# Reordering the opening of a fused attention and feed-forward kernel: an earlier first norm, feed-forward products in place of fills, three loads on GpSimd's queue

## The chip, the cores and the metric

The kernel runs on one core of a Trainium2 chip. The metric is device time in microseconds of one execution. A core has five engines that run independently and meet through semaphores: TensorE (matmuls, "PE" in the profile, with its weight loads as "PEld"), VectorE ("DVE"), ScalarE ("ACT"), GpSimd ("POOL") and SyncE ("SP", which only issues DMAs here). Each engine executes its own instructions in the order in which the program lists them. An instruction that has to wait holds up everything behind it on its engine, and nothing on the others.

## The reference

For 8 batches of 12 heads, 448 tokens and 64 features per head, q and k are divided by their norms, and attention is taken over the cosines:

```python
q_n = q / (np.linalg.norm(q, axis=-1, keepdims=True) + 1e-06)
k_n = k / (np.linalg.norm(k, axis=-1, keepdims=True) + 1e-06)
scores = np.matmul(q_n, k_n.transpose(0, 1, 3, 2)) / tau      # tau = 0.1
attn = softmax(scores)
x = np.matmul(attn, v)                  # (8, 12, 448, 64) -> (3584, 768)
h = x @ w_in                            # 768 -> 2048
g = np.maximum(0.01 * h, h)
out = g @ w_out                         # 2048 -> 768
```

Inputs and outputs are float32; products are taken in bf16.

## The kernel before, in words

**Slots.** A pair of heads is the unit of the first two batches: slots 0 to 5 are the six pairs of batch 0, slots 6 to 11 those of batch 1. From slot 12 (`OLD`) on, slots come two to a unit (one for q, one for k) in another layout. Every slot goes through the same steps, each on its own engine:

1. `load_qk(s)` brings q and k into a buffer `qk_h` (four buffers, so slot s takes the one of slot s-4). Slots below 12 need four DMAs (lines 142 to 145), later ones two (line 134). All are on SyncE's queue, apart from three at the very start.
2. `squares(s)` on GpSimd (line 206 for slots below 12, line 199 later), `sums(s)` on VectorE (220, 214), `roots(s)` on ScalarE (227, 228), `normalise(s)` on VectorE (236, 237, then 253 or 243), which writes `qn`.
3. `transposes(s)`: for slots below 12 seven matmuls on TensorE (267) and a copy on VectorE (308).
4. `scores(s, key tiles)`: matmuls (329) and one exponential per key tile on ScalarE (338).
5. For two slots together (a quad j): `totals(j)` sums the exponentials on TensorE and inverts the sums on ScalarE (360, 361), `products(j, e)` multiplies by v (349), and `scale(j, e)` on VectorE (380) writes two of the six 128-row tiles of `xT`. `attend(j)` is all three.

`hold(x)` is a one-element copy on GpSimd (585). It keeps GpSimd's next squares behind the named `qn`.

**Feed-forward.** `first(c, m)` makes one 128-row tile of h from six matmuls (`KT` = 6, line 474) and an activation on ScalarE (483). `second(c, ts, half)` needs 16 matmuls with one half of w_out's columns (505). `work[0]` lists the 16 `first` and 6 `second` groups of the first chunk; `feed_groups(0, n)` issues the next n of them between attention steps. Of its last six groups three use w_out's first half and then three its second half.

**Order.** The order is written out by hand: a loop over the six slots of batch 0 (line 621), then straight lines for slots 6 to 15 (from line 688), then a planned stream. Before it stand a few lines for slot 0 (589 to 617). `fill(n)` issues n matmuls of 512 columns on a constant tile (576), whose results nobody reads.

**GpSimd's queue.** GpSimd computes the squares, and it also issues the loads that change float32 to bf16: `load_v(j)` (160), `load_v_rem(b)` (168, one DMA per head position), `load_w_in(i)` (105, quarters), `load_w_out(half)` (111). Such a load is an instruction in GpSimd's order of work like any other.

**PSUM.** `banks(n)` hands out one or two of eight banks, the longest unused first; a bank with a name in `kept` isn't handed out until `given_back`.

Of the kernel before, what the change touches and what calls it, by code (L numbers as in the profile page):

```python
# [16 lines left out]
def kernel(  # L17
# [10 lines left out]
    nc = tc.nc  # L28
# [8 lines left out]
    NPAIR = H // 2  # L37
    NSLOT = B * NPAIR
    NQ = NPAIR // 2
# [83 lines left out]
            x[:, 512:896].rearrange("p (h t d) -> p h t d", h=2, d=D),  # L123
        )

    def load_qk(s, engs=(nc.sync, nc.sync), rem_engs=None):
        if s >= NSLOT:
            return
        whole = ldp.tile([128, 14 * D], F32, name="qk_h")
        if s >= OLD:  # L130
            u, which = divmod(s - OLD, 2)
            for w, pair in enumerate(UNITS[u][1]):
                b, h0 = pair // NPAIR, 2 * (pair % NPAIR)
                nc.sync.dma_start(
                    out=whole[64 * w : 64 * w + 64],
                    in_=(q, k)[which][b, h0 : h0 + 2].rearrange("h (p t) d -> (h p) (t d)", t=14),
                )
            raw[s] = whole
            return
        b, h0 = s // NPAIR, 2 * (s % NPAIR)  # L140
        q_h, k_h = halves(whole)
        engs[0].dma_start(out=q_h[:, :, 0:3], in_=main(q, b, h0, 2))
        engs[1].dma_start(out=k_h, in_=main(k, b, h0, 2))
        for i, (x, eng) in enumerate(zip((q, k), rem_engs or engs)):
            eng.dma_start(
                out=q_h[64 * i : 64 * i + 64, :, 3],
                in_=x[b, h0 : h0 + 2, MAIN:S].rearrange("h p d -> p h d"),
            )
        raw[s] = (q_h, k_h)
# [315 lines left out]

    begun = {}

    def first(c, m, lo=0, hi=KT):
        c0, n = chunk_cols(c)
        if c not in hT:  # L470
            hT[c] = htp.tile([128, MT, 512], BF16, name="hT")
        pm = begun.pop((c, m)) if lo else banks(1)
        for kt in range(lo, hi):
            nc.tensor.matmul(  # L474
                out=pm[:, :n],
                lhsT=w_in_sb[:, kt, m * 128 : (m + 1) * 128],
                rhs=xT[c // 2][:, kt, c0 : c0 + n],
                start=(kt == 0), stop=(kt == KT - 1),
            )
        if hi < KT:  # L480
            begun[c, m] = pm
            return
        nc.scalar.activation(out=hT[c][:, m, :n], in_=pm[:, :n], func=AF.Prelu, alpha=0.01)  # L483

    osb = {}
# [112 lines left out]
        )  # L598
    roots(0)
    squares(1, (nc.scalar, gp))  # L600
    sums(1, (1,))
    normalise(0)
    load_qk(4)
    load_v_rem(0, range(2))
    hold(qn[0][:, 6, 0, 0:1])
# [15 lines left out]
    for s in range(NPAIR):  # L621
        j = s // 2 - 1 if s >= 2 else None
        even = s % 2 == 0
        n = s + 2 if 0 < s < NPAIR - 2 else None
        last = s == NPAIR - 1
        if s == 1:
            roots(2)
        scores(s, (0,))
        if j is not None and not even:
            products(j, 1)  # L630
        scores(s, (1,))
        fill(2)
        if n:
            sums(n, (0,))
        if not last:
            normalise(s + 1)
            load_qk(s + 5)
        if late:
            scale(late.pop(), 1)
        if j is not None and not even:  # L640
            scale(j, 0)
        if last:
            load_w_out(0)
        else:
            hold(qn[s + 1][:, 6, 0, 0:1])
        squares(s + 3)
        if s == 0:
            sums(2)
            load_v_rem(0, range(2, 4))
        if s in (1, 2):  # L650
            load_v(s)
        if last:
            load_v(NQ)
            load_v_rem(1)
        elif s != 1:
            load_w_in(max(s - 1, 0))
        if n:
            sums(n, (1,))
        scores(s, (2,))
        if not even or s == 0:  # L660
            fill(2)
        if n and not even:
            roots(n)
        if not even:
            scores(s, (3,))
        if j is not None and even:
            totals(j)
        if not last:
            transposes(s + 1)
        if j is not None and even:  # L670
            products(j, 0)
        if not even or s == 0:
            fill(2)
        if n and even:
            roots(n)
        if j is not None and not even:
            late.append(j)

    def attend(j):
# [8 lines left out]
    deals["apart"] = False  # L688
    deals["width"] = 64
    s, j = NPAIR, NQ - 1  # L690
    scale(late.pop(), 1)
    totals(j)
    sums(s)
    po = banks(2)
    for e in range(2):
        products(j, e, po[:, e])
    for m in range(2):
        first(0, m, 0, KT - 2)
    for e in range(2):
        scale(j, e)  # L700
    roots(s)
    for m in range(2):
        first(0, m, KT - 2)
    work[0] = work[0][2:]
    normalise(s)
    load_qk(s + 4)
    hold(qn[s][:, 6, 0, 0:1])
# [2 lines left out]
    feed_groups(0, 1)  # L710
    transposes(s)
    roots(s + 1)
    feed_groups(0, 1)
    normalise(s + 1)
    load_qk(s + 5)
    sums(s + 2)
# [4 lines left out]
    roots(s + 2)  # L721
    normalise(s + 2)
    hold(qn[s + 2][:, 6, 0, 0:1])
    squares(s + 4)
    load_v(s // 2 + 1)
    load_w_out(1)
# [4 lines left out]
    transposes(s + 2)  # L731
    roots(s + 3)
    normalise(s + 3)
    load_qk(s + 6)
    sums(s + 4)
    feed_groups(0, 2)
    scores(s + 1, (2, 3))
# [23 lines left out]
    feed_groups(0, 1)  # L761
    transposes(s + 4)
    sums(s + 5)
    feed_groups(0, 2)
    roots(s + 5)

    scores(s + 3, (0, 1, 2))
# [7 lines left out]

    scores(s + 4, (0, 1))
    scores(s + 3, (3,))
    load_qk(s + 9)
    settle(s + 6)
    sums(s + 7)  # L780
    feed_groups(0, 1)
# [3 lines left out]
    scores(s + 5, (0, 1))  # L785
    feed_groups(0, 1)
    attend(NQ + 1)
    load_qk(s + 10)
    settle(s + 7)
    sums(s + 8)  # L790

# [146 lines left out]
```

## Time and profile before

| | |
|---|---|
| median of 3 runs | 422.45 us (421.23, 422.45, 1805.44) |
| the profiled execution | 421.03 us |
| its span, first to last instruction | 419.2 us |
| TensorE busy | 410.0 us, 98% of the span |
| ScalarE, VectorE, GpSimd busy | 254.4, 223.0, 116.6 us |
| granted TensorE clock | 1.000 of full speed |
| first half of w_out, issue to landing | 24.5 us |
| second half of w_out, issue to landing | 20.7 us |

The profile shows one execution. Busy times are those in which an engine executes an instruction. A row of the timeline reads: start and duration in us, engine, line, operation, tile written and tiles read, how many in a row; in brackets the idle time of the engine just before and what ended it. A row of the list of waits reads: who waited, for whom, us in total, how often, the longest. The one run of 1805.44 us lies far from the others, and the profiled execution agrees with the two lower ones.

### The profile page before, as it was taken

To read this page: it belongs to the slowest core of one execution; us is meant where nothing else is said; L and a number is where in the kernel's file an instruction comes from. 1 tells how busy PE (TensorE), PEld (TensorE's weight loads), DVE (VectorE), ACT (ScalarE), POOL (GpSimd) and SP (SyncE) were. 2 spreads that over 40 slices of the span, in tenths; PEclk is the share of its full clock that TensorE was granted. 3 is DMA by queue.
4 is the path that set the end of the run, shared out by engine and by line. 5 is a ranking of instruction groups with operands and counts; after the bars stand their busy time and mean duration, and the time that the engine had idled before them with its cause. 6 is when DMAs were issued, how large, how long until landed. Compare 5 with 4: busy or idle time off the path is not lost.

```text
span 419.2 us, 11328 instructions
## 1 busy us (share of the span) xinstructions
PE 410.0 (98%) x4797; PEld 211.9 (51%) x4797; DVE 223.0 (53%) x385; ACT 254.4 (61%) x430; POOL 116.6 (28%) x149
## 2 busy tenths in 40 slices
PE   7899999999999999999999999999999999999996
PEld 2334555544455555544455555554445555654563
DVE  6886886874687555864583864464621311210021
ACT  4896877377766686757874778547764364014300
POOL 3877472431433223512430523131210000000000
PEclk9999999999999999999999999999999999999999
DMA  6999999485387932884275592743441100010021
GB/s 164 173 232 231 221 236 225 107 238 113 84 196 224 215 79 57 203 205 115 60 181 160 126 233 74 170 121 89 90 89 52 66 38 3 38 77 0 2 75 75
DMA packets 41906, 53.82 MB, mean 128 GB/s; under 512 B 12544, under 2 KB 32256, under 8 KB 41856
## 3 DMA queue, kind: packets, MB, share of 16 engines
q1 hardware_dynamic: 25680, 40.88, 34.9%
q0 software_dynamic: 15488, 11.80, 19.8%
q8 instruction: 37, 0.61, 0.6%
q10 hardware_dynamic: 688, 0.43, 0.4%
q14 instruction: 13, 0.11, 0.1%
HBM read 45.61 MB, written 11.01 MB: 135 GB/s over the span
## 4 chain that ended last, share of the span: by engine, by line
PE 89%; DMA 3%; DVE 3%; ACT 3%; issue 0%; SPq 0%; DVEq 0%
PE ps L505 35%; PE ps L474 33%; PE ps L425 9%; PE ps L400 7%; PE ps L349 3%; DMA qk_h<-in_q_dram 3%; DVE qn L253 2%; ACT pe L338 1%; PE ps L329 1%; PE ps L576 1%; DMA qk_h<-in_k_dram 1%; PE ps L267 1%; ACT ss L227 0%; ACT hT L483 0%; ACT norms L228 0%
## 5 line engine op out<-in xcount | busy, mean ns | idle before, releaser
L505 PE MATMUL ps<-w_out_sb,hT 128*128 128x384 bf16 x896 | 151.3, 326 | 0.4 <-DVE xT L380 0.4
L474 PE MATMUL ps<-xT,w_in_sb 128*128 128x384 bf16 (+1 forms) x768 | 150.8, 353 | 0.0
L406 ACT ACTIVATE pe<-ps 128x896 bf16<-128x896 f32 x126 | 108.9, 915 | 44.6 <-PE ps L400 44.6
L505 PEld LDWEIGHTS <-hT 128*128 128x128 bf16 x896 | 85.5, 98 | 65.2 <-issue 10.3
L474 PEld LDWEIGHTS <-w_in_sb 128*128 128x128 bf16 x768 | 72.8, 98 | 74.0 <-issue 9.2
L483 ACT ACTIVATE hT<-ps 128x384 bf16<-128x384 f32 (+1 forms) x128 | 67.6, 550 | 54.1 <-PE ps L474 53.6
L516 DVE COPY osb<-ps 128x384 f32<-128x384 f32 (+1 forms) x56 | 30.8, 551 | 101.3 <-PE ps L505 100.3
L199 POOL TENSOR_TENSOR sq<-qk_h 128x896 f32<-128x896 f32 x36 | 60.5, 1681 | 3.3 <-DMA qk_h<-in_k_dram 3.2
L585 POOL CAST seen<-qn 128x1 f32<-128x1 bf16 x46 | 8.9, 193 | 173.7 <-DVE qn L243 168.0
L243 DVE TENSOR_TENSOR qn<-qk_h,r 128x896 bf16<-128x896 f32 x36 | 42.5, 1182 | 1.4 <-DVE r L237 0.2
L338 ACT ACTIVATE pe<-ps 128x896 bf16<-128x896 f32 x42 | 35.9, 915 | 2.4 <-PE ps L329 2.3
L214 DVE TENSOR_REDUCE ss<-sq 128x14 f32<-128x896 f32 x36 | 37.3, 1037 | 0.0
L400 PE MATMUL ps<-qkT 64*32 64x448 bf16 x1008 | 36.5, 353 | 0.0
L236 DVE TENSOR_REDUCE r<-norms 128x14 f32<-128x28 f32 x48 | 8.6, 179 | 49.2 <-ACT norms L228 48.7
L227 ACT ACTIVATE ss<-ss,tiny 128x14 f32<-128x14 f32 x48 | 14.7, 306 | 28.5 <-DVE ss L214 25.6
L450 DVE TENSOR_TENSOR xT<-ps,rb 128x448 bf16<-128x448 f32 x32 | 18.4, 617 | 22.3 <-PE ps L425 21.2
L289 DVE STREAM_TRANSPOSE tt<-qn 128x448 f32<-128x448 f32 x36 | 29.6, 821 | 0.9
L425 PE MATMUL ps<-pe,vq 64*32 64x448 bf16 x1008 | 27.0, 349 | 0.0
L206 POOL TENSOR_TENSOR sq<-qk_h 128x384 f32<-128x384 f32 (+1 forms) x21 | 20.8, 1009 | 14.9 <-DMA qk_h<-in_k_dram 14.9
L400 PEld LDWEIGHTS <-qkT 64*32 64x32 bf16 x1008 | 13.2, 91 | 19.3 <-issue 14.5
L425 PEld LDWEIGHTS <-vq 64*32 64x32 bf16 x1008 | 14.5, 93 | 8.0 <-issue 0.3
L253 DVE TENSOR_TENSOR qn<-qk_h,r 128x512 bf16<-128x512 f32 (+1 forms) x24 | 18.2, 798 | 0.4
(52 smaller groups left out, 215.8 us busy)
## 6 DMA issues: line engine op xcount, KB each, us to landing
qk_h<-in_q_dram SPq DMA_DIRECT2D x36, 224.0 KB, 4.3
qk_h<-in_k_dram SPq DMA_DIRECT2D x36, 224.0 KB, 4.4
out_dram<-osb SPq DMA_DIRECT2D x20, 384.0 KB, 3.0
qkT<-tt SPq DMA_DIRECT2D x72, 56.0 KB, 3.3
qkT<-tt SPq DMA_DIRECT2D x36, 112.0 KB, 3.5
vq<-in_v_dram POOLq DMA_DIRECT2D x16, 224.0 KB, 5.1
w_in_sb<-in_moe_w_in_dram POOLq DMA_DIRECT2D x4, 768.0 KB, 11.1
w_out_sb<-in_moe_w_out_dram POOLq DMA_DIRECT2D x2, 1536.0 KB, 22.6
```

Source lines behind the costliest of these rows:

```text
L199: gp.tensor_tensor(sq, raw[s], raw[s], op=ALU.mult)
L214: nc.vector.tensor_reduce(ss[s], sqs[s].rearrange("p (t d) -> p t d", d=D), axis=AX.X, op=ALU.add)
L243: nc.vector.tensor_tensor(qn[s].rearrange("p m d e -> p m e d"), raw[s].rearrange(f"p ({t[1:-1]} d) -> p m e d", e=n, d=D), r.rearrange(f" ...
L289: nc.vector.transpose(out=to.rearrange(("p g (c m) -> p m g c", "p g (m c) -> p m g c")[which], m=7), in_=qn[s].bitcast(F32).rearrange("p ...
L338: nc.scalar.activation(out=dst, in_=sc[:, :, :S], func=AF.Exp, scale=inv_tau)
L400: nc.tensor.matmul(out=sc[32 * strip : 32 * strip + 32, a, :S], lhsT=x[rows, c0 : c0 + 32], rhs=x[rows, 0:S], start=True, stop=True,)
L406: nc.scalar.activation(out=pq[u, i], in_=sc[:, :, :S], func=AF.Exp, scale=inv_tau)
L425: nc.tensor.matmul(out=po[32 * strip : 32 * strip + 32, w, :S], lhsT=weights, rhs=pq[us[x if two else 0], i][rows, a, :], start=(i == 0), ...
L474: nc.tensor.matmul(out=pm[:, :n], lhsT=w_in_sb[:, kt, m * 128 : (m + 1) * 128], rhs=xT[c // 2][:, kt, c0 : c0 + n], start=(kt == 0), stop= ...
L483: nc.scalar.activation(out=hT[c][:, m, :n], in_=pm[:, :n], func=AF.Prelu, alpha=0.01)
L505: nc.tensor.matmul(out=po2[:, :HALF], lhsT=hT[c][:, m, ts * 128 : (ts + 1) * 128], rhs=w_out_sb[:, m, half * HALF : (half + 1) * HALF], st ...
L516: nc.vector.tensor_copy(out=o[:, half * HALF : half * HALF + cut], in_=po2[:, :cut])
```

## The change

In the lines for slot 0 and in the loop over batch 0:

- `normalise(0)` stands ahead of `sums(1, (1,))`, both on VectorE.
- `scores(s, (0,))` stands ahead of `roots(2)` in step s = 1, and `sums(2)` in step 0 stands behind `transposes(1)`.
- In step s the loop lists the load of slot s+4 instead of s+5 (step 0 still loads slot 5, step 1 none, step 5 loads slot 9).
- w_in's second quarter is loaded in step 1, ahead of v's third load, instead of in step 2, behind it.
- In step 5 two fills of two matmuls each go. In their place stand matmuls of the first two feed-forward groups: first the k tiles 0 and 2 of both groups, then the tiles 1 and 3. `first` takes a list of k tiles for that, and its bank is kept until the group is complete. `scale(j, 1)` is issued directly behind `scale(j, 0)`.

In the straight lines behind the loop:

- Groups 2 and 3 are begun where groups 0 and 1 were, and all four are completed together. Two calls of `feed_groups` are shortened by one group each, so that the number of groups stays 22.
- The load of slot 12 is issued by GpSimd instead of SyncE, behind `hold` of slot 8. There too stand the load of v for quad 3 and the four `load_v_rem(1)`, which were in step 5; all of them are ahead of `squares(10)`.
- The loads of slots 15 and 16 are issued by GpSimd instead of SyncE, in their old places in the program.

```diff
-    def first(c, m, lo=0, hi=KT):
+    def first(c, m, kts=range(KT)):
...
-        pm = begun.pop((c, m)) if lo else banks(1)
-        for kt in range(lo, hi):
+        if (c, m) in begun:
+            pm, done = begun.pop((c, m))
+        else:
+            pm, done = banks(1, (c, m, "begun") if len(kts) < KT else None), 0
+        for i, kt in enumerate(kts):
...
-                start=(kt == 0), stop=(kt == KT - 1),
+                start=(done + i == 0), stop=(done + i == KT - 1),
...
+    normalise(0)
     sums(1, (1,))
-    normalise(0)
...
+        scores(s, (0,))
         if s == 1:
             roots(2)
-        scores(s, (0,))
...
-            load_qk(s + 5)
+        if s == 0:
+            load_qk(5)
+        elif s > 1:
+            load_qk(s + 4)
...
         if last:
+            scale(j, 1)
             load_w_out(0)
...
         if s == 0:
-            sums(2)
             load_v_rem(0, range(2, 4))
...
-        if last:
-            load_v(NQ)
-            load_v_rem(1)
-        elif s != 1:
-            load_w_in(max(s - 1, 0))
+        if s < 2:
+            load_w_in(s)
+        elif 2 < s < NPAIR - 1:
+            load_w_in(s - 1)
...
         scores(s, (2,))
-        if not even or s == 0:
+        if last:
+            for m in range(2):
+                first(0, m, (0, 2))
+        elif not even or s == 0:
             fill(2)
...
             transposes(s + 1)
+        if s == 0:
+            sums(2)
...
+        if last:
+            for m in range(2):
+                first(0, m, (1, 3))
+        elif not even or s == 0:
             fill(2)
...
-    for m in range(2):
-        first(0, m, 0, KT - 2)
+    for m in range(2, 4):
+        first(0, m, range(KT - 2))
...
-    for m in range(2):
-        first(0, m, KT - 2)
-    work[0] = work[0][2:]
+    for m in range(4):
+        first(0, m, range(KT - 2, KT))
+    work[0] = work[0][4:]
...
     roots(s + 1)
-    feed_groups(0, 1)
     normalise(s + 1)
...
     hold(qn[s + 2][:, 6, 0, 0:1])
+    load_qk(s + 6, eng=gp)
+    load_v(NQ)
+    load_v_rem(1)
     squares(s + 4)
     load_v(s // 2 + 1)
     load_w_out(1)
...
     normalise(s + 3)
-    load_qk(s + 6)
     sums(s + 4)
...
     sums(s + 5)
-    feed_groups(0, 2)
+    feed_groups(0, 1)
     roots(s + 5)
...
-    load_qk(s + 9)
+    load_qk(s + 9, eng=gp)
...
-    load_qk(s + 10)
+    load_qk(s + 10, eng=gp)
```

In the straight lines s is 6, so s + 6 is slot 12, s + 9 is slot 15, s + 4 is slot 10.

## The prediction

> **What bounds the kernel now.** I read the page's busy times first, then who TensorE waits for, then GpSimd's order of work between 36 and 70 us, then the landings of single loads.
>
> ```profile
> PE 410.0 (98%) x4797; PEld 211.9 (51%) x4797; DVE 223.0 (53%) x385; ACT 254.4 (61%) x430; POOL 116.6 (28%) x149
> ...
> PE 89%; DMA 3%; DVE 3%; ACT 3%; issue 0%; SPq 0%; DVEq 0%
> ```
>
> TensorE is busy for all but 9.2 us. What can be gained is thus small whatever is moved: less TensorE work, or fewer of those 9.2 us. Work added anywhere else costs only where TensorE comes to wait.
>
> ```profile
> PE ps L576 <- DVE pe L559: 1.6, 1, 1.6
> PE ps L267 <- DVE qn L253: 1.0, 1, 1.0
> PE ps L329 <- ACT pe L338: 0.8, 3, 0.3
> PE ps L329 <- ACT norms L228: 0.8, 1, 0.8
> PE ps L329 <- DVE qkT L308: 0.6, 2, 0.3
> PE ps L505 <- DVE xT L380: 0.4, 1, 0.4
> ```
>
> All of these but the last lie before 28 us. After that TensorE hardly waits, but it is not far ahead of the others. The transposes of slots 8, 9 and 10 (L267 at 47.66, 51.84, 55.40) take some 0.64 us from their first matmul to the next group, where those of slot 7 took 0.39: their second half starts when DVE's qn ends (55.79 for slot 10, matmuls at 55.85). So the chain load, squares (GpSimd), sums, roots, qn runs without slack there, and GpSimd sits in it:
>
> ```profile
> 39.22 0.81 POOL L160 DMA_DIRECT2D v_b<-in_v_dram  x1
> 40.03 2.49 POOL L168 DMA_DIRECT2D v_rem<-in_v_dram  x4
> 42.51 0.55 POOL L585 CAST seen<-qn 128x1 f32<-128x1 bf16 x1
> 45.23 1.82 POOL L206 TENSOR_TENSOR sq<-qk_h 128x512 f32<-128x512 f32 x2 [2.17 <-DMA qk_h<-in_k_dram]
> 48.14 0.18 POOL L585 CAST seen<-qn 128x1 f32<-128x1 bf16 x1 [1.09 <-DVE qn L253]
> 50.40 2.53 POOL L206 TENSOR_TENSOR sq<-qk_h 128x512 f32<-128x512 f32 x2 [2.08 <-DMA qk_h<-in_k_dram]
> 52.88 0.82 POOL L160 DMA_DIRECT2D v_b<-in_v_dram  x1
> 53.69 1.16 POOL L111 DMA_DIRECT2D w_out_sb<-in_moe_w_out_dram  x1
> 55.86 0.18 POOL L585 CAST seen<-qn 128x1 f32<-128x1 bf16 x1 [1.00 <-DVE qn L253]
> 56.04 1.82 POOL L206 TENSOR_TENSOR sq<-qk_h 128x512 f32<-128x512 f32 x2
> 58.04 0.82 POOL L160 DMA_DIRECT2D v_b<-in_v_dram  x1 [0.18 <-issue]
> ```
>
> The third load of v and the four v_rem of 39.22 to 42.52 stand where GpSimd then idles 2.17 us for slot 9. The change puts them, and slot 12's two loads, between 48.33 and the squares of slot 10. The last row holds the second point: the trace has the queue's wait for that load ending at 57.53, and the first half of w_out landed at 57.51 (24.5 us after its issue at 32.98). GpSimd's loads use eight completion semaphores in turn, in every one of the 24 loads whose semaphores I followed, and a load waits until the one eight places before it has landed. v's sixth load stands eight behind w_out's first half.
>
> **Part by part.**
>
> *First norm earlier.* DVE idled 1.04 us until 7.26 for GpSimd's squares; norms(0) were ready at 6.81. So DVE's run to the copy of qkT(0) starts 0.4 earlier, and the first scores start near 9.9 instead of 10.35. Then sums(2) goes behind the copy of qkT(1): that copy starts at 12.55 instead of 13.69 and the second pair's scores at 13.2 instead of 14.36. But roots(2) now follow the first exponential (13.6 to 14.5) and end at 15.0 instead of 14.36; qn(2) ends at 16.66 (was 16.45), sums(3) at 17.13 (was 16.92), roots(3) start at 17.15 (was 17.17), and the fourth exponential of this pair, behind them on ScalarE, at 17.6 (was 17.64). The next one starts at 18.46, was 18.57. I take 0.1 us; the ends are 0 and 2.2 (0.8, 0.8 and 0.6 of the waits above).
>
> *Loads of slots 6 to 9 one place later in the program.* Nothing: SyncE issues only these loads there, in the same order, when the buffer's last reader is done (slot 6 at 16.52, qn(2) ends at 16.45).
>
> *w_in's second quarter ahead of v's third load.* GpSimd's transfers land in order of issue without a pause from 16 to 74 us (25.44, 27.26, 30.06, 34.78, 40.10, 43.92, 57.51). Exchanging the third and fourth gives w_in near 32.0 and v at 34.8; their readers come at 33.6 and 35.1. Zero, and up to 1 us of waiting that the later wait would cover.
>
> *Fills become products.* In the last step two fills of 0.54 us (33.56 to 34.10) go, and eight matmuls of 0.163 (16 in 2.61) come: 0.22 us more. ScalarE's last exponential ends at 34.60 and held the last part of the totals to 34.68, so this is nearly covered. Afterwards these eight are saved: 1.08 us less TensorE work in all. By scores(6) six groups are done instead of five, and the groups taken out later give them back, so TensorE is some 0.1 us early until 56 and 1.1 after it. scale(1,1) runs in the same place on DVE (31.70). The kept banks are ones long read.
>
> *GpSimd, 48 to 53 us.* After hold(8) (48.33) come two loads of slot 12, v (0.82) and four v_rem (2.49). No row has the slot's load on GpSimd; the nearest are vq (0.62, also 64 partitions) and SyncE's 0.49; at most w_out's 1.2. With 0.62 each: 4.55 us. The squares of slot 10 start at 52.9, not 50.40, last 1.83 beside an idle DVE (2.53 before), and end at 54.7 instead of 52.93: +1.8. Sums, roots, qn follow at their old distances: qn(10) ends at 57.6, the transposes at 57.8 instead of 56.03. One group (0.98) less stands behind them, so scores(9) start at 58.8 (was 58.07).
>
> *GpSimd's next loads.* v's fifth load is now eight behind w_out's first half and goes out at 57.5 at the earliest; w_out's second half is eight behind slot 12's first load, which lies behind w_out in GpSimd's transfers. Its 224 KB need less than v's 2.68 (57.51 to 60.19) and more than a v_rem's 0.3; by bytes read (v is read as 393 KB) 1.6, so 59.1. w_out's issue takes 1.2, hold(10) 0.2: the squares of slot 11, behind all this on GpSimd, start at 60.5 instead of 56.04, **+4.45**. From there by the old distances: squares end 62.3, sums 62.9, roots 63.55, qn(11) at 65.9 (it ran beside the next squares, as before), transposes(11) end at 66.15 instead of 61.93. TensorE finishes the group ahead of them at 62.1 and waits. **+4.2 us**; all later work is TensorE's own, back to back, and keeps it.
>
> *Slots 15 and 16 on GpSimd.* They land behind w_out's second half: near 78 and 80 instead of 68.77 and 74.23. Their squares come at 76.64 + 4.2 = 80.8 and 84.9. Zero. w_out itself: slot 12 until 60.6, v 63.3, v_rem 64.5, v 66.8 (their old steps of 2.68, 1.18, 2.27), then 10.7 as before or less, 77.5 at most; read at 74.44 + 4.2 = 78.6. Zero, with 1.1 us to spare.
>
> A rule to set beside the wait: TensorE would stand idle some 3.3 us before transposes(11). At the start the trace shows what follows idleness: weight loads of the fill 0.43 us apart from 2.00 to 4.13, and 0.215 later, so half speed for the first 2.9 us. The Trainium skill (TensorE: Matmul & The Clock Gate, "Part 1: The HAM clock gate") says that about 3.4 us of idling halves the clock until some 3.4 us of work have passed; by an estimate from it 1.7 us would come on top. The trace of before has no later gap that long (the granted clock is 1.00 throughout). This is a rival below, priced from the rows.
>
> **The sum.** The profiled execution took 421.03 (span 419.2, 1.8 around it). 421.03 + 4.2 = 425.2. Ordinary runs took 421.23 and 422.45, so I add 0.2: **425.4**.
>
> **The rivals.**
>
> 1. *The clock falls after the wait.* For: 3.3 us of idling. Against: no such row after the start. Price: 2.9 us at half speed, 1.45: 426.9.
> 2. *The eight-place wait is not what holds GpSimd* (w_out's half lands by 55). Then only the seven loads count: squares(11) at 57.8, transposes(11) end at 63.2, +1.3: 422.5. Against: the queue's wait that ended at 57.53.
> 3. *Not slower: the chain of slots 10 and 11 keeps out of TensorE's way*, because slots 9 to 11 land earlier and GpSimd finds its loads done. What is left is 1.08 + 0.1 less: 420.0. Against: slot 10's squares have to follow hold(8) and seven issues in GpSimd's order.
> 4. *w_out's second half comes late.* It decides from a landing at 78.6. At the first half's pace (43.92 to 57.51, 13.6 us) it lands at 80.4, +1.8, and slots 15 and 16 behind it may add 2: 427 to 429; only a pace slower still passes 431.
> 5. *The new order isn't in force* (the same queues and waits as before): 421.2.
>
> **Chances.** Forecast 0.54, rival 1 0.18, rival 2 0.10, rival 3 0.08, rival 4 0.08, rival 5 0.02. Range 421.5 to 429: below the forecast it takes in rival 2 and the short end of slot 12's transfer (0.3 instead of 1.6: 423.9), above it rivals 1 and 4 and the long end (2.7 and 1.2 for each of its issues: 427); outside are rivals 3 and 5 and the worst of 4. Of these only the worst of 4 is slower by over 2% (8.4 us, about what a measurement of this kernel can tell from no change): 0.04; faster by that much would need nearly all of the 9.2 us: 0.01.
>
> **What would show it.** In the changed profile: GpSimd's squares of slot 10 start near 52.9 with no wait for a load; a load of v starts at 57.5 to 58 and w_out's second half near 59; squares(11) near 60.5; TensorE has a wait of 1.5 to 2 us at L267 for DVE's qn near 57 and one of 3 to 4 near 65; the first norm's DVE work starts at 6.85; TensorE is within 0.5 us of before at 42. If w_out's first half lands much before or after 57.5, the sum moves with it, one for one. The prediction is wrong if GpSimd's loads wait on something other than the eighth before, or if slot 12's load lands well after 60.

## The result and the profile after

The changed kernel took 424.98 us (median of 12 runs, 423.68 to 426.28), the kernel before 421.8 us. The ratio is **1.0072, with an interval of [1.0057, 1.0087]**: some 3 us slower. The profiled execution took 424.75 us with a span of 423.0 us, 3.72 us above the 421.03 of before. That execution of before lies 0.8 us below the median of its 12 runs, so a difference of under 1 us between a trace and the one of before tells little of the usual time. One run of before (1805.44) and one of an experiment below (1078.92) lie far outside all the others and are left out of the ratios.

The first view is the page of the changed kernel: the busy times, and the chain that ended last by engine.

```profile
PE 411.1 (97%) x4793; PEld 212.5 (50%) x4793; DVE 221.6 (52%) x385; ACT 254.2 (60%) x430; POOL 118.7 (28%) x155
...
PE 84%; DMA 10%; POOL 2%; DVE 1%; issue 1%; SPq 1%; ACT 0%; POOLq 0%; DVEq 0%
```

TensorE has four instructions less (four fills of 512 columns went) but is busy 1.1 us longer. A stretch of 3.41 us at half clock, below, accounts for some +1.7 us. At the start, where the clock rises at 5.79 us instead of 4.50, the same 22 fills take 6.98 us instead of 6.33. The four fills that went account for -1.08. In the chain DMA went from 3% to 10%, and GpSimd now has a share: the chain of the changed kernel passes through loads and through GpSimd's order of work.

For whom TensorE waits, in the changed kernel (waiting line, releaser, us in total, times, longest):

```profile
PE ps L329 <- DVE qkT L308: 2.9, 4, 2.0
PE ps L329 <- ACT pe L338: 1.6, 5, 0.4
PE ps L581 <- DVE pe L564: 1.6, 1, 1.6
PE ps L267 <- DVE qn L253: 1.0, 2, 0.6
```

Line 581 is the wait for the fill's constant tile at the start, 1.6 as before. New is one wait of 2.0 us at line 329, the scores, for VectorE's copy of qkT. The wait for qn at line 267 is as long in sum as before (1.0), but it lies elsewhere now: 0.62 of it stands right before the transposes of slot 11.

GpSimd's timeline of the changed kernel, 45 to 62 us (start, duration, engine, line, operation, tiles; in brackets the idle time before and what ended it):

```profile
44.99 1.82 POOL L206 TENSOR_TENSOR sq<-qk_h 128x512 f32<-128x512 f32 x2 [4.51 <-DMA qk_h<-in_k_dram]
48.13 0.18 POOL L590 CAST seen<-qn 128x1 f32<-128x1 bf16 x1 [1.32 <-DVE qn L253]
48.68 1.14 POOL L134 DMA_DIRECT2D qk_h<-in_q_dram  x2 [0.36 <-POOL seen L590]
49.80 0.81 POOL L160 DMA_DIRECT2D v_b<-in_v_dram  x1
50.58 2.49 POOL L168 DMA_DIRECT2D v_rem<-in_v_dram  x4
53.08 1.84 POOL L206 TENSOR_TENSOR sq<-qk_h 128x512 f32<-128x512 f32 x2
57.33 0.81 POOL L160 DMA_DIRECT2D v_b<-in_v_dram  x1 [2.41 <-DMA w_out_sb<-in_moe_w_out_dram]
58.40 1.16 POOL L111 DMA_DIRECT2D w_out_sb<-in_moe_w_out_dram  x1 [0.26 <-DMA qk_h<-in_q_dram]
59.55 0.20 POOL L590 CAST seen<-qn 128x1 f32<-128x1 bf16 x1
59.69 1.82 POOL L206 TENSOR_TENSOR sq<-qk_h 128x512 f32<-128x512 f32 x2
```

The squares of slot 10 start at 53.08 (50.40 before) with no wait for a load ahead of them. Then GpSimd stands for 2.41 us, until w_out's first half has landed (at 56.80, by the landings of single loads; v's load starts 0.53 us later, as it does before the change, at 58.04 after 57.51), and 0.26 us until slot 12's first load has (58.11). Only then come w_out's second half, the hold and the squares of slot 11: 59.69, where before they came at 56.04. Both brackets name a transfer that the waiting instruction neither reads nor writes; it is the one eight loads before it on this queue.

TensorE's timeline of the changed kernel over the same time:

```profile
53.53 0.57 PE L329 MATMUL ps<-qkT 64*64 64x448 bf16 x8
56.09 0.38 PE L329 MATMUL ps<-qkT 64*64 64x448 bf16 x4 [1.99 <-DVE qkT L308]
56.41 1.58 PE L477 MATMUL ps<-xT,w_in_sb 128*128 128x384 bf16 x6
57.78 0.95 PE L267 MATMUL ps<-id,qn 128*128 128x128 bf16 x7
58.52 2.07 PE L477 MATMUL ps<-xT,w_in_sb 128*128 128x384 bf16 x6
60.52 0.76 PE L329 MATMUL ps<-qkT 64*64 64x448 bf16 x12
61.22 2.78 PE L510 MATMUL ps<-w_out_sb,hT 128*128 128x384 bf16 x16
64.61 0.81 PE L267 MATMUL ps<-id,qn 128*128 128x128 bf16 x7 [0.62 <-DVE qn L253]
65.35 0.75 PE L349 MATMUL ps<-pe,ones 128*32 128x448 bf16 x12
...
88.19 0.76 PE L400 MATMUL ps<-qkT 64*32 64x448 bf16 x24
```

The same three places in the kernel before:

```profile
61.38 0.63 PE L267 MATMUL ps<-id,qn 128*128 128x128 bf16 x7
61.93 0.75 PE L349 MATMUL ps<-pe,ones 128*32 128x448 bf16 x12
...
84.83 0.76 PE L400 MATMUL ps<-qkT 64*32 64x448 bf16 x24
```

In the changed kernel TensorE waits twice, 1.99 us in the middle of slot 8's scores and 0.62 us before the transposes of slot 11. These end 3.4 us later than before (65.35 against 61.93), and what follows keeps the distance: the first matmuls of line 400 start at 88.19 (84.83 before, +3.36), TensorE's last one ends at 418.98 (415.62, +3.36). The remaining 0.4 us of the profiled difference lie behind ScalarE's last copy, in the last store. The wait of 1.99 us stands where it does because the third key tile needs a PSUM bank that VectorE's copy of slot 9's transposes has to empty (slot 8's scores do not read what it copies), and that copy stands behind sums(10) on VectorE, which wait for the late squares of slot 10.

The group at 58.52 takes 2.07 us where six such matmuls otherwise take 1.14. The table of windows of the changed kernel, 56 to 60 us (window, length, busy us and instructions of PE, PEld, DVE, ACT, POOL, then granted clock, DMA share, GB/s), shows why:

```profile
56.00:60.00 4.00, 3.91 (x22) 2.33 (x22) 2.25 (x6) 3.27 (x6) 2.41 (x4) 0.62 1.35 199
```

The granted clock is 0.62 in this window. Its records are at half speed from 56.99 to 60.41.

### The profile page after: what moved, and what is told of

The parts are those of the page before. It is cut to its first block, busy times and chain, and to the rows that moved or that the text cites. A ratio compares the mean times of both kernels' runs of the same rounds, so it can differ in the third digit from the quotient of the medians.

```text
span 423.0 us, 11317 instructions
## 1 busy us (share of the span) xinstructions
PE 411.1 (97%) x4793; PEld 212.5 (50%) x4793; DVE 221.6 (52%) x385; ACT 254.2 (60%) x430; POOL 118.7 (28%) x155
## 4 chain that ended last, share of the span: by engine, by line
PE 84%; DMA 10%; POOL 2%; DVE 1%; issue 1%; SPq 1%; ACT 0%; POOLq 0%; DVEq 0%
PE ps L510 35%; PE ps L477 31%; PE ps L425 9%; PE ps L400 7%; DMA w_out_sb<-in_moe_w_out_dram 5%; DMA qk_h<-in_k_dram 4%; PE ps L349 2%; POOL sq L206 1%; DMA qk_h<-in_q_dram 1%; SPq L145 1%; DVE qn L253 0%; POOL w_in_sb L105 0%; PE ps L329 0%; POOL v_b L160 0%; POOL v_rem L168 0%
## 5 line engine op out<-in xcount | busy, mean ns | idle before, releaser
L477 PE MATMUL ps<-xT,w_in_sb 128*128 128x384 bf16 (+1 forms) x768 | 152.5, 355 | 0.0
L206 POOL TENSOR_TENSOR sq<-qk_h 128x384 f32<-128x384 f32 (+1 forms) x21 | 19.9, 965 | 16.4 <-DMA qk_h<-in_k_dram 16.3
L329 PE MATMUL ps<-qkT 64*64 64x448 bf16 (+1 forms) x132 | 12.9, 359 | 4.8 <-DVE qkT L308 2.9
```

The lines of the kernel that those rows point to most:

```text
L477: nc.tensor.matmul(out=pm[:, :n], lhsT=w_in_sb[:, kt, m * 128 : (m + 1) * 128], rhs=xT[c // 2][:, kt, c0 : c0 + n], start=(done + i == 0), ...
```

## The experiments

The theory to test was that of the prediction: the queue part of the change makes the loss, by two things on GpSimd, the seven issues ahead of the squares of slot 10, and above all the wait for the load eight places before. The rivals were the clock, the opening (first norm, fills, w_in) and the late transfers.

**The changed kernel with the queue of before** (slots 12, 15 and 16 back on SyncE, v and v_rem back in step 5; opening and products as changed):

```diff
+        if last:
+            load_v(NQ)
+            load_v_rem(1)
...
     hold(qn[s + 2][:, 6, 0, 0:1])
-    load_qk(s + 6, eng=gp)
-    load_v(NQ)
-    load_v_rem(1)
     squares(s + 4)
...
     normalise(s + 3)
+    load_qk(s + 6)
     sums(s + 4)
...
-    load_qk(s + 9, eng=gp)
+    load_qk(s + 9)
...
-    load_qk(s + 10, eng=gp)
+    load_qk(s + 10)
```

> The changed kernel with GpSimd's queue as it was before: slots 12, 15 and 16 loaded by SyncE, v's load for quad 3 and the four v_rem back in step 5. Theory (GpSimd's queue is what costs): the 3.4 us of the changed profile go, and what is left is 1.1 us less TensorE work and an opening worth 0 to 0.6 us more: 420.3 to 421.5, ratio to before 0.997 to 1.000; squares of slot 11 near 56, no half-clock stretch. Rival A (the opening's reordering costs as much as the queue): 422.5 or more, ratio above 1.002. Rival B (w_out's second half now ends last): TensorE waits up to 1 us near 73.5, 421.5 to 422.

Measured: ratio 1.0007 [0.9995, 1.0019]. The loss is gone, and the gain that the theory expected (0.997 to 1.000) did not appear. TensorE's timeline of this kernel shows two waits for qn, before the second half of slot 9's transposes and before slot 11's:

```profile
53.18 0.34 PE L267 MATMUL ps<-id,qn 128*128 128x128 bf16 x3 [0.70 <-DVE qn L253]
...
61.62 0.81 PE L267 MATMUL ps<-id,qn 128*128 128x128 bf16 x7 [0.40 <-DVE qn L253]
```

They add up to 1.10 us, and the transposes of slot 11 start at 61.62 (61.38 before). The squares of slot 11 come at 56.70 here.

**The queue part alone, in the kernel before:**

```diff
-        if last:
-            load_v(NQ)
-            load_v_rem(1)
-        elif s != 1:
+        if not last and s != 1:
             load_w_in(max(s - 1, 0))
...
     hold(qn[s + 2][:, 6, 0, 0:1])
+    load_qk(s + 6, eng=gp)
+    load_v(NQ)
+    load_v_rem(1)
     squares(s + 4)
...
     normalise(s + 3)
-    load_qk(s + 6)
...
-    load_qk(s + 9)
+    load_qk(s + 9, eng=gp)
...
-    load_qk(s + 10)
+    load_qk(s + 10, eng=gp)
```

> The kernel before with the queue part of the change alone: slot 12, v's load for quad 3 and the four v_rem on GpSimd ahead of the squares of slot 10, slots 15 and 16 on GpSimd. Opening, fills and feed-forward groups as before. Theory (the queue part makes the whole loss): v's fifth load goes out when w_out's first half has landed, squares(11) near 59.7, transposes of slot 11 end at 65.3 or a little later, since one more group stands ahead of them and may run at half clock: 424.7 to 426.2, ratio 1.007 to 1.0105. Rival (queue and opening add up): 423 to 424.3, ratio below 1.006.

Measured: 424.11, 424.45 and 425.84, ratio 1.0076 [1.0055, 1.0097]. The profiled execution was the one of 1078.92 us, so no line of it is used. With the run before this shows that the queue part makes the whole loss: alone it gives 1.0076, everything but it gives 1.0007, both together 1.0072.

**Slot 12's load back on SyncE, all else as changed.** v's fifth load is then six places behind w_out's first half instead of eight. Five issues, not seven, stand ahead of the squares of slot 10:

```diff
     hold(qn[s + 2][:, 6, 0, 0:1])
-    load_qk(s + 6, eng=gp)
+    load_qk(s + 6)
     load_v(NQ)
     load_v_rem(1)
     squares(s + 4)
```

> The changed kernel with slot 12 alone back on SyncE; v and the four v_rem stay ahead of the squares of slot 10. v's fifth load is then six, not eight, loads behind w_out's first half. Theory (the wait for the load eight places before is the larger part): that load goes out at 53 to 54 without a wait, squares(10) start near 51.7, squares(11) near 57, TensorE waits 1 us or less: 421 to 422, ratio 0.999 to 1.001. Rival (GpSimd's time for the loads is the price): five sevenths of the loss stays, 423.7 or more.

Measured: 422.95 us, ratio 1.0022 [1.001, 1.0035], between the two expectations. GpSimd's timeline of this kernel:

```profile
52.67 1.98 POOL L206 TENSOR_TENSOR sq<-qk_h 128x512 f32<-128x512 f32 x2
54.60 0.81 POOL L160 DMA_DIRECT2D v_b<-in_v_dram  x1
55.41 1.17 POOL L111 DMA_DIRECT2D w_out_sb<-in_moe_w_out_dram  x1
57.57 0.18 POOL L590 CAST seen<-qn 128x1 f32<-128x1 bf16 x1 [1.00 <-DVE qn L253]
57.75 1.82 POOL L206 TENSOR_TENSOR sq<-qk_h 128x512 f32<-128x512 f32 x2
```

The squares of slot 10 are only 0.41 us earlier than in the changed kernel, but v's load follows them at once, without a wait, and the squares of slot 11 start at 57.75 instead of 59.69: 1.94 us earlier. The first matmuls of line 400 follow by the same amount (86.26 against 88.19, 1.93). So two loads less on the queue take away about two thirds of the loss (0.0050 of 0.0072 in the ratios, 2.1 us). With them go three things at once: the wait on the eighth load before, two issues ahead of the squares of slot 10, and the stretch at half clock, which this trace does not have (the granted clock is 1.00 from 6 us on). This run does not part them. What is left against the run with the old queue (1.0022 against 1.0007, intervals that overlap) fits the five issues that still delay the squares of slot 10; in the traces it is 1.05 us (86.26 against 85.21). TensorE's timeline of this kernel has a shorter wait at the same place:

```profile
55.82 0.38 PE L329 MATMUL ps<-qkT 64*64 64x448 bf16 x4 [0.98 <-DVE qkT L308]
```

It ends only 0.27 us earlier than in the changed kernel (55.82 against 56.09); the rest of the difference is that TensorE came to these scores 0.74 us later (54.27 against 53.53).

**The squares of slot 10 ahead of the seven loads:**

```diff
     hold(qn[s + 2][:, 6, 0, 0:1])
+    squares(s + 4)
     load_qk(s + 6, eng=gp)
     load_v(NQ)
     load_v_rem(1)
-    squares(s + 4)
     load_v(s // 2 + 1)
     load_w_out(1)
```

> The changed kernel with the squares of slot 10 ahead of the seven loads on GpSimd. Theory (the wait for w_out's landing decides): squares(10) start near 50.4, but v's fifth load still goes out near 57.3 and squares(11) near 59.7; TensorE's wait at the scores near 54 to 56 goes, the one before the transposes of slot 11 grows to 2 to 4 us: the time stays, 424 to 425.5, ratio 1.005 to 1.009. Rival (the seven issues ahead of squares(10) are the price): 422 to 423.

Measured: 426.74 us, ratio 1.011 [1.0091, 1.0128], slower than the changed kernel and than either expectation. The squares of slot 10 start at 50.16, as before the change, and TensorE goes through slots 8 to 10 without the long wait. But w_out's second half goes out at 58.44 and the squares of slot 11 start at 59.74, just as late as in the changed kernel. GpSimd's timeline of this kernel:

```profile
56.91 0.79 POOL L160 DMA_DIRECT2D v_b<-in_v_dram  x1
58.44 1.16 POOL L111 DMA_DIRECT2D w_out_sb<-in_moe_w_out_dram  x1 [0.74 <-DMA qk_h<-in_q_dram]
```

The seven issues now end at 56.91, and w_out's first half has landed by then (55.94), so v's fifth load does not wait for it. What holds w_out's second half is the landing of slot 12's first load, eight places before it (58.15, 58.11 in the changed kernel). The delay of slot 10 and that of slot 11 are thus not a sum: the later one, the landing, sets the squares of slot 11 with or without the delay of slot 10. TensorE's timeline and the table of windows:

```profile
64.66 0.97 PE L267 MATMUL ps<-id,qn 128*128 128x128 bf16 x7 [4.46 <-DVE qn L253]
```

```profile
60.00:64.00 4.00, 0.20 (x2) 0.00 (x0) 2.39 (x5) 1.77 (x4) 3.98 (x4) 0.89 1.37 194
64.00:68.00 4.00, 3.34 (x35) 1.67 (x39) 3.06 (x5) 2.36 (x6) 2.90 (x5) 0.50 1.32 204
68.00:72.00 4.00, 4.00 (x44) 1.67 (x37) 2.35 (x5) 1.94 (x3) 0.04 (x1) 0.76 1.35 235
```

The waiting is now one piece of 4.46 us, and the clock is at half from 63.11 to 69.94, 6.8 us. From the start of slot 11's transposes to the first matmul of line 400 it takes 25.50 us, against 23.58 in the changed kernel. This 1.9 us lies on the path.

**The same, with the wait filled** by 20 matmuls on the constant tile (4.3 us of work that nobody reads; 19 of them are in the trace):

```diff
     roots(s + 6)
+    fill(20)
     transposes(s + 5)
     attend(NQ)
```

> The kernel with squares(10) first, plus 20 matmuls on a constant tile (4.3 us) where TensorE waits 4.5 us for the qn of slot 11. Nothing else is moved. Theory (the long wait halves TensorE's clock, and the 6.8 us at half clock that follow cost about 2 us): the half-clock stretch after 63 goes, the transposes of slot 11 come at the same time, 64.7 to 65.2, the first quad matmul near 88.3 instead of 90.2: 424.6 to 425.4, ratio 1.006 to 1.0085. Rival (the stretch at half clock costs nothing, or the added matmuls are late themselves): 426.5 or more, ratio 1.011 or more.

Measured: 426.23 us, ratio 1.0104 [1.0086, 1.0121]. TensorE's timeline of this kernel:

```profile
60.34 4.26 PE L581 MATMUL ps<-pe 128*128 128x512 bf16 x19
65.89 0.81 PE L267 MATMUL ps<-id,qn 128*128 128x128 bf16 x7 [1.28 <-DVE qn L253]
```

The granted clock stays at 1.00 through the stretch, and the way from slot 11's transposes to line 400 is 23.58 us again: 1.9 us won. But slot 12's load landed 1.2 us later in this execution (59.37 against 58.15), w_out's second half went out at 59.66 and the transposes started 1.2 us later. The time is only 0.5 us lower, and the four runs of each overlap. So the price of the half clock is shown inside the trace; the time of the whole, above the 424.6 to 425.4 expected, does not confirm its size.

**The squares of slot 11 ahead of v's fifth load and w_out's second half:**

```diff
     squares(s + 4)
-    load_v(s // 2 + 1)
-    load_w_out(1)
     sums(s + 3)
...
     squares(s + 5)
+    load_v(s // 2 + 1)
+    load_w_out(1)
     load_v(s // 2 + 2)
```

> The changed kernel with v's fifth load and w_out's second half behind the squares of slot 11 on GpSimd; the seven loads stay ahead of squares(10). Theory: squares(11) start right after the qn of slot 10, near 58, transposes of slot 11 end near 63.3 instead of 65.35; w_out's second half is issued near 61, lands near 73 to 75, read at 75.8: 422.3 to 423.3, ratio 1.001 to 1.004. Rival (slot 11's squares do not hold TensorE): 424.5 to 425.5.

Measured: 424.49 us, ratio 1.0064 [1.0047, 1.0081], while less was expected. The squares of slot 11 do start at 57.66 as expected, and so this step of the theory holds. TensorE's timeline of this kernel shows where the gain went:

```profile
55.76 0.38 PE L329 MATMUL ps<-qkT 64*64 64x448 bf16 x4 [1.99 <-DVE qkT L308]
```

This wait is as long as in the changed kernel, since the squares of slot 10 are as late. Half clock follows it, from 56.85 to 60.26, and TensorE itself reaches the transposes of slot 11 only at 63.44, 0.76 later than where slot 12's load was on SyncE (62.68, a wait of 0.40 included). There the second half of them waits another 0.52 us for qn, and they end at 64.62, only 0.73 us earlier than in the changed kernel (65.35). So taking the squares of slot 11 out from behind the wait, with the seven issues left in place, gains next to nothing: the second limit, TensorE itself, stands close behind the first. In the changed kernel the late qn(11) covers the slow stretch; here it does not. That the clock explains this kernel's time is not settled: one of its four runs had a mean clock of 1.000 and took 424.86.

**Slots 15 and 16 back on SyncE, all else as changed:**

```diff
-    load_qk(s + 9, eng=gp)
+    load_qk(s + 9)
...
-    load_qk(s + 10, eng=gp)
+    load_qk(s + 10)
```

> The changed kernel with slots 15 and 16 back on SyncE. Theory (they cost and bring nothing): w_out's second half lands later than 72.4, near 74 to 75, still ahead of its reader near 77.8: same time as the changed kernel, ratio to before 1.0055 to 1.009. Rival (with the two slots beside it w_out's second half comes too late): TensorE waits for it near 78, ratio above 1.010.

Measured: 425.2, 425.55, 425.59 and 428.76, ratio 1.0111 [1.0082, 1.014], in the range of the rival. Its mechanism is not in the trace, though: in the profiled execution w_out's second half landed at 74.94 and was read at 78.49 without a wait, slot 11's transposes started at 65.30. So moving these two loads back takes nothing of the loss away; whether moving them back to SyncE makes it a little worse is open, because the interval meets that of the changed kernel.

**The first norm alone, in the kernel before:**

```diff
+    normalise(0)
     sums(1, (1,))
-    normalise(0)
...
+        scores(s, (0,))
         if s == 1:
             roots(2)
-        scores(s, (0,))
...
         if s == 0:
-            sums(2)
             load_v_rem(0, range(2, 4))
...
             transposes(s + 1)
+        if s == 0:
+            sums(2)
```

> The kernel before with the reordering of the first norm alone (normalise(0) ahead of sums(1), the second pair's scores ahead of roots(2), sums(2) behind the second transposes). The changed profile has its first scores 0.35 us earlier but the transposes of slot 3 0.6 later. Theory (what the opening wins or loses is taken up by the later waits for qn): ratio 0.999 to 1.0015, 421.2 to 422.2; transposes of slot 3 start 0.2 to 0.5 us later than 20.71. Rival (the opening is a gain of its own): ratio 0.9985 or less.

Measured: ratio 1.0002 [0.9992, 1.0013]. The transposes of slot 3 start at 21.09, 0.38 later than before (20.71), and nothing of it reaches the end.

**The changed kernel without the wait on w_out, with v and v_rem back in step 5 and the first norm undone** (slot 12 on SyncE, slots 15 and 16 on GpSimd; the core of the edit):

```diff
     squares(1, (nc.scalar, gp))
-    normalise(0)
     sums(1, (1,))
+    normalise(0)
...
+        if last:
+            load_v(NQ)
+            load_v_rem(1)
...
     hold(qn[s + 2][:, 6, 0, 0:1])
-    load_qk(s + 6, eng=gp)
-    load_v(NQ)
-    load_v_rem(1)
     squares(s + 4)
...
     normalise(s + 3)
+    load_qk(s + 6)
     sums(s + 4)
```

> The changed kernel with slot 12 on SyncE and v and v_rem back in step 5 (slots 15 and 16 stay on GpSimd), and without the first norm's reordering: normalise(0), roots(2) and sums(2) in their places of before. What is left of the change is products for fills, w_in's quarter ahead of v's third load, and slots 15 and 16. Theory (the chain load, squares, qn sets the pace up to slot 11, so that 1.08 us less TensorE work turns into waits): TensorE still waits for qn before the transposes of slots 9 to 11, the first quad matmul comes at 84.3 to 85: 421 to 421.9, ratio 0.9985 to 1.0005. Rival (the reordering at the start is what hid the gain): 420.7 or less, ratio 0.9975 or less.

Measured: 422.51 us, ratio 1.0025 [1.0013, 1.0037], a miss. TensorE's timeline of this kernel:

```profile
59.71 2.76 PE L510 MATMUL ps<-w_out_sb,hT 128*128 128x384 bf16 x16 [1.99 <-DMA w_out_sb<-in_moe_w_out_dram]
```

Here w_out's first half was issued at 36.59 and landed at 59.66, and TensorE waited 1.99 us for the data itself, with the old place of v's loads. In the changed kernel this half landed at 56.80, in the one before at 57.51. The traces of the other runs sort this landing by the queue of slot 12's load. In the five with slot 12 on GpSimd, behind w_out, it lies between 55.94 and 57.20; in the eight with slot 12 on SyncE, beside w_out, between 57.02 and 59.66, and in the five of these eight that issue it about as late as the changed kernel (35.45 to 36.59, against 36.16) at 57.56 or later. The pair that differs by slot 12's queue alone has 56.80 (changed) against 58.46. So taking slot 12's load off SyncE fits as what brings the landing forward; one trace for each kernel does not prove it, and the size of this run's 59.66 stays open. So this run says nothing on the first norm; the run of the first norm alone does.

**w_in's second quarter ahead of v's third load, alone in the kernel before:**

```diff
-        elif s != 1:
-            load_w_in(max(s - 1, 0))
+        elif s < 2:
+            load_w_in(s)
+        elif s > 2:
+            load_w_in(s - 1)
```

> The kernel before with w_in's second quarter alone moved ahead of v's third load. Theory: slot 7's load lands near 33 instead of 28.73 and w_out's first half is issued near 36 instead of 33, but it lands no later than 58, so that the time stays: ratio 0.999 to 1.001. Rival (the later issue delays w_out's landing, and the first groups of the second product wait for it): 422.2 to 423.5, ratio 1.0015 to 1.004.

Measured: ratio 1.0000 [0.9991, 1.001]. GpSimd's timeline and then TensorE's, of this kernel:

```profile
33.76 1.82 POOL L206 TENSOR_TENSOR sq<-qk_h 128x512 f32<-128x512 f32 x2 [3.10 <-DMA qk_h<-in_k_dram]
35.53 0.79 POOL L105 DMA_DIRECT2D w_in_sb<-in_moe_w_in_dram  x1
36.33 1.18 POOL L111 DMA_DIRECT2D w_out_sb<-in_moe_w_out_dram  x1
```

```profile
59.14 2.77 PE L505 MATMUL ps<-w_out_sb,hT 128*128 128x384 bf16 x16 [0.65 <-DMA w_out_sb<-in_moe_w_out_dram]
```

The exchange of two loads on GpSimd's queue makes SyncE's load of slot 7 late: the squares of slot 7 wait 3.10 us for it and start at 33.76 (30.42 before), and everything behind them on GpSimd, w_out's first half among it, goes out 3.4 us later (36.33 against 32.98). SyncE itself issued slot 7's loads within 0.3 us of before (20.51 to 22.73 against 20.33 to 22.52). w_out's first half landed at 59.10, past the 58 that the theory allowed, and TensorE waits 0.65 us for it, as the rival had it. Slot 11's transposes start at 61.75 (61.38 before), and their second half waits 0.51 us for qn. In the median of the time nothing of this is seen.

**Two fills put back** into the first of these kernels (1.1 us more TensorE work in step 5):

```diff
             for m in range(2):
                 first(0, m, (1, 3))
+            for _ in range(2):
+                fill(2)
```

> The changed kernel with GpSimd's queue as before, and the two fills put back in step 5 behind the products that replaced them: 1.1 us more TensorE work at the same place. Theory (TensorE had that much idle time before the transposes of slot 11): as without them, 421.5 to 422.3, ratio 1.000 to 1.0015. Rival (TensorE's own work sets the time): 1 us more, 422.7 or more, ratio 1.003 or more.

Measured: ratio 1.0001 [0.9991, 1.0011], where the same kernel without them has 1.0007 [0.9995, 1.0019]. 1.1 us more work of the engine that is busy for 98% of the span adds nothing to the time. In the traces slot 11's transposes start 0.41 us later (62.03 against 61.62), less than half of what was added, and in both they wait for qn first (0.47 and 0.40 us).

**The two fills of step 5 taken out of the kernel before, nothing in their place:**

```diff
-        if not even or s == 0:
+        if not last and (not even or s == 0):
             fill(2)
```

(at both places of the loop)

> The kernel before without the two fills of step 5 and with nothing in their place: 1.1 us less TensorE work, the same results. Theory (the load chain sets the pace until slot 11's transposes): 421.1 to 421.9, ratio 0.9985 to 1.0005. Rival (TensorE's own work sets the time, as the prediction's sum for the not slower case has it): 420.3 to 420.7, ratio 0.9965 to 0.9975.

Measured: ratio 0.9997 [0.9986, 1.0008]. For whom TensorE waits, in this kernel:

```profile
PE ps L267 <- DVE qn L253: 1.4, 2, 0.9
PE ps L329 <- ACT pe L338: 1.0, 4, 0.3
...
PE ps L505 <- DVE xT L380: 0.5, 1, 0.5
PE ps L349 <- ACT pe L338: 0.4, 1, 0.4
```

Against before, the wait for qn grows from 1.0 to 1.4, those for the exponentials from 0.8 to 1.0 at line 329 and by 0.4 at line 349, that for xT from 0.4 to 0.5, and the wait for the first norms goes from 0.8 to 0.6: 0.9 us in all, of the 1.08 that the fills took. Slot 11's transposes start at 61.47 (61.38 before). So TensorE's work between 33 and 61 us may be 1.1 us more or less, and the time stays.

No version is faster than both kernels by more than the measurement tells.

## Why the prediction was right, point by point

**The sum.** 425.2 was worked out for the profiled execution, 424.75 came; 425.4 for ordinary runs, 424.98 came. The mechanism is the one that was named, with some of its terms mis-sized. That the time for ordinary runs is so close is in part luck: the sum took 421.2 for the kernel before, whose 12 runs have a median of 421.8, and +4.2 for the change, where the medians give +3.2. The two errors cancel to 0.4.

**GpSimd's next loads**, the step that carries the forecast, is confirmed by the changed trace, in which both waits stand where they were said to, and by the run with slot 12 on SyncE, in which they are gone. v's fifth load went out at 57.33 (57.5 worked out), the squares of slot 11 came at 59.69 (60.5), qn(11) ended at 65.02 (65.9) and slot 11's transposes ended at 65.35 (66.15). Instead of +4.2 it was +3.4. The size was off in two places: w_out's first half landed at 56.80, not 57.51, and slot 12's first load 1.31 us after it, not 1.6. Both are transfer times; for the second the ends of the range had 0.3 and 2.7. Against this, a held load starts only some time after the landing (0.53 and 0.29 us here), which the sum had at nothing. What the wait is worth by itself is not shown: with slot 11's squares out from behind it and all else as changed, the loss stays (ratio 1.0064), since TensorE's own delay is nearly as long.

**GpSimd, 48 to 53 us.** Right in GpSimd's times: 4.40 us from the first issue to the squares of slot 10 (4.55 worked out), which start at 53.08 (52.9); qn(10) ends at 57.78 (57.6). Wrong in where TensorE would feel it: not at line 267 near 57 for qn(10), but earlier, in slot 8's scores, by a PSUM bank that VectorE empties behind sums(10). The prediction followed the chain squares, sums, roots, qn and left out what else stands behind sums on VectorE. It cost nothing in the sum because the end was set by qn(11). Where qn(11) comes earlier, as in the run with slot 11's squares first, this wait and the slow stretch behind it set the end.

**Fills become products** failed as a term. The prediction had TensorE 1.1 us ahead after 56 us. The runs with fills out, with fills back and with the old queue show that these 1.08 us turn into waits, for qn and for ScalarE's exponentials (0.4 and 0.6 us more in the run with the fills out): up to slot 11's transposes TensorE does not set the pace, although it is busy for nearly all of that time. In this sum the error did not show, as TensorE's lead was to become a wait before slot 11's transposes in any case.

**First norm earlier** was taken as −0.1. Its first half came as worked out (scores at 10.00 instead of 10.35); further on the transposes of slot 3 are later, by 0.38 us in the run of this part alone. In the time it is nothing. TensorE was to be within 0.5 us of before at 42, and just was not: 42.54 against 41.97 at slot 6's scores, with some 0.27 of it from first loads that landed later in this execution.

**w_in's second quarter**: the two landings were right (32.16 and 34.53; 32.0 and 34.8 worked out), and the price was right at zero. The step missed that slot 7's load, on another queue, would land at 33.44 instead of 28.73 and hold up GpSimd, so that w_out's first half went out 3.2 us later (36.16). That it landed at 56.80 all the same, before the 57.51 of the earlier issue, is why the forecast's largest term survived. The prediction gave no reason for this, so it is luck; the landings sorted above suggest that the change itself helped, by taking slot 12's load off SyncE.

**Slots 15 and 16, w_out's second half**: zero, as said, with more room than worked out. w_out landed at 72.39 (77.5 at most) and was read at 77.80; slots 15 and 16 landed between 74.86 and 77.68 (78 and 80).

**The rivals.** *The eight-place wait is not the holder* fell by the run with slot 12 on SyncE. *Not slower* fell by the time, and its 420.0 can't be reached in any case, since the 1.08 us are not there to be had. *w_out's second half late* and *the new order isn't in force* fell by the trace. *The clock falls after the wait* came true in part. It fell after the first wait, not the one before slot 11's transposes. In the profiled execution it cost nothing: it ate into the time in which TensorE would have waited for qn(11), so that only 0.62 us of that wait is left. For the other runs this is not settled. Of the 12, the two with a mean clock of 0.998 or more took 423.68 and 423.90; the ten with 0.994 to 0.996 have a median of 425.45. The queue part alone (424.11 and 424.45 at 0.999 or more, 425.84 at 0.995) looks the same, the kernel with slot 11's squares first does not (424.86 at 1.000, 424.93 at 0.994). A run whose loads land earlier may have both the higher clock and the shorter time, so this does not make the clock the cause. With the trace of one execution only, it can't be said where those lose it. If it is the clock, part of the measured loss comes from a term that the sum of the forecast had at nothing.

## What to carry to other kernels

Before a load is moved on a queue, count the loads between it and the slow one ahead: here a load issued by GpSimd waited until the one eight places before it had landed, and two loads less on the queue took away two thirds of the loss. An engine that computes and issues loads passes such a wait on to its arithmetic, even if the data that are waited for are needed by nobody yet. And an engine at 98% busy need not be the bound of each stretch: put a microsecond of idle work into the stretch, or take one out, and see whether the time follows.

## What was not expected of the hardware

**A wait of 2 us can halve TensorE's clock.** After a wait of 1.99 us the granted clock was at half from 56.99 to 60.41 in the changed kernel, and from 56.85 to 60.26 where slot 11's squares came first: 3.41 us each time. In the kernel that waits 4.46 us (60.20 to 64.66) it was at half for 6.83 us, from 63.11 on, twice that. After a wait of 0.98 us (slot 12 on SyncE) it stayed at 1.00, and so it did after the 1.99 us for w_out's data. So about 2 us is neither always enough nor always too short. The traces fit steps of 3.413 us that run from the clock's rise at the start: 5.79 plus 15 steps is 56.99, 5.65 plus 15 is 56.85, and 5.09 plus 17 is 63.11. By this count the changed kernel's whole wait (54.10 to 56.09) lies in one step, the one from 53.58 to 56.99, at whose end the clock falls. In the kernel that waited for w_out's data (rise at 4.73) a step ends at 59.34, in the middle of the wait: 1.62 us lie before it and 0.37 behind it, and the clock stays. The Trainium skill (TensorE: Matmul & The Clock Gate, "Part 1: The HAM clock gate") gives a free-running window of 3413 ns, and puts the halving after at least one idle window of about 3.4 us. The lengths of 3.41 and 6.83 us agree with that window, and a window that runs freely fits that equal waits had unequal effects. If an idle window is one without any work, that does not agree: in the 3.41 us that end at 56.99 in the changed kernel TensorE worked until 54.1 and from 56.09 on, some 1.4 us in all.

**Loads on different queues delay each other by several us.** w_in's second quarter, issued by GpSimd one place earlier, put the landing of SyncE's load of slot 7 from 28.73 to 33.44 in the changed kernel. In the kernel before with this exchange alone the squares that need it started at 33.76 instead of 30.42, with the time unchanged.
